# One addition of a weight conversion: VectorE or GpSimd

## The chip, the cores and the metric

The kernel runs on one core of one Trainium2 chip. The metric is the device time of one execution in microseconds, the median of several runs. A core has five engines that run side by side, each through its own list of instructions in order: TensorE (PE, matrix products; PEld is its weight load), VectorE (DVE), ScalarE (ACT), GpSimd (POOL) and SyncE (SP, which here starts the DMA transfers). They meet only through semaphores and memory. SBUF is the on-chip memory that all of them reach, PSUM the memory that TensorE writes its products to.

## What is computed

A gated linear attention and a two-layer network behind it (batch 4, 8 heads, 768 steps, head width 48; network width 384, 2048 inside):

```
for t in range(S):
    state = alpha[:, :, t, :, None] * state + k_t v_t^T
    y[:, :, t] = q_t state
x = y as (3072 tokens, 384)
h = x @ w_in
g = max(0.01 * h, h)
out = g @ w_out
```

The two weights arrive in double precision (64-bit words). The kernel has to turn them into numbers that TensorE can multiply.

## The kernel before, in words

**Products in two halves.** TensorE multiplies in a reduced format, fp32r. Every operand is therefore kept as a high half and a low half: the value rounded to fp32r, and what the rounding left. A product x·w is the sum of three: high·high, low·high and high·low. For the weights the halves of slice f (128 of the 2048 inner columns, 16 slices) lie in one tile `w{f}`, 128 x 768 each: 384 columns of `w_in` and 384 of `w_out`.

**Converting a weight slice.** `converting(f, ordered)` (L240) is a generator. The raw 64-bit words of the slice come by DMA into a tile `raw`. Then, for a slice with `ordered`, each on 128 x 768 elements:

- L259, ScalarE: the top word is scaled as if it were a float.
- L262, ScalarE: a cast of it whose result holds the sign (`signs`).
- L265, VectorE: top word shifted and joined with the sign: `bits`, a float.
- L273, ScalarE: the high half of `w`, rounded from `bits`.
- L277, VectorE: the exponent of `bits` alone, into `pw`.
- L279, VectorE: `bits` minus the high half, in place.
- L281, VectorE: the low word times the exponent, into `rest`, which is `pw` under another name.
- L284, VectorE: `rest` + `val` (which is `bits`) gives the low half of `w`.

Between two of these steps stands a `yield`, so that the caller can put other work between them. `pw` has one buffer (NPW = 1), `bits` two (NBITS = 2), `raw` four.

**Written order.** `put(ordered, eng, op)` (L231) keeps a list for VectorE and one for ScalarE. Each ordered instruction is told to stand behind the last one of its list (`issue_after`), so the order on these two engines is written out by hand. Everything else is put in order by the framework's scheduler, which works from its own estimate of when each instruction could start. The first three slices are converted without that order, in the attention part at the beginning; slices 3 to 15, thirteen, are ordered.

**The items.** The network's work is cut into items (i, f): `ffn_in` takes 384 tokens (block i) through slice f, nine matmuls into a PSUM tile `ph` (two buffers), and makes `gh` and `gl`, the halves of g; `ffn_out`, three items later (LAG = 3), multiplies them with the `w_out` part, nine matmuls. Inside `ffn_in` the steps on the other engines are: L712, ScalarE, t = 0.01 · ph; L715, VectorE, t = max(ph, t); L717, ScalarE, gh; L721, VectorE, gl = t - gh. Blocks 0 and 1 go through the slices together: (0,0), (1,0), (0,1), (1,1) and so on, a pair for each slice. While they do, each pair carries one conversion. The steps are handed out like this (L840 to L845): in an item of block 0, between L717 and L721, L259 of one slice, the last step (L284) of a second and L265 of a third; in an item of block 1, L273 and L277 ahead of L715, then L279 ahead of L721, and L262 and L281 after it. Seen on VectorE, a pair is thus: L281, L715, L284, L265 (next slice), L721, L277, L715, L279, L721, and again L281.

The first matmul of block 0 that uses the low half of slice f comes in the pair after the one in which L284 wrote it.

**Attention between.** The attention of the first nine units (a unit is 128 steps of one batch row) is done at the beginning; the other fifteen are spread between the items by `pace` (L798), which hands out steps by written-down costs. A few of their steps fall among the conversions: transposes (L314), running products (`tensor_tensor_scan`, L339 and L346; through `vector` at L292), and GpSimd's small copies L345 and L351. GpSimd also masks scores (L415) and scales states (L422, a `tensor_tensor` on 192 columns).

Of the kernel before, what the change touches and what calls it, by code (L numbers as in the profile page):

```python
# [17 lines left out]
ALU = mybir.AluOpType  # L18
# [6 lines left out]
def gated_linear_attn_ffn(ctx, tc, q, k, v, alpha, w_in, w_out, out):  # L25
    nc = tc.nc
# [72 lines left out]
    state, vals_sb, rest = rest[:B], rest[B:B + NV], rest[B + NV:]  # L99
# [15 lines left out]
    made = {}  # L115
# [3 lines left out]
    def behind(*key):  # L119

        return tc.issue_after(made[key].ins) if key in made else nullcontext()
# [109 lines left out]
    def put(ordered, eng, op, *args):  # L231

        if not ordered:
            return op(*args)
        line = lines[eng]
        with tc.issue_after(line[-1].ins) if line else nullcontext():
            line.append(op(*args))
        return line[-1]

    def converting(f, ordered=False):  # L240

        if f >= NF:
            return
        raw = jobs.pop(f)
        w_sb[f] = cst.tile([P, 2, 2 * DM], F32R, name=f"w{f}")
        hi, lo = w_sb[f][:, HIGH, :], w_sb[f][:, LOW, :]
        if not f64:
            val = raw[:, :, 0:P].bitcast(F32)
            hi, lo = (t.rearrange("p (g f) -> p g f", f=P) for t in (hi, lo))
            nc.scalar.copy(hi, val)  # L250
            made["w", f] = nc.vector.tensor_tensor(lo, val, hi.bitcast(F32), ALU.subtract)
            return
        words = raw.rearrange("p g (f w) -> p (g f) w", w=2)
        top, low = words[:, :, 1], words[:, :, 0]
        bits = cvp.tile([P, 2 * DM], I32, name="bits", bufs=NBITS)
        val = bits.bitcast(F32)

        with nullcontext() if lines["ACT"] else behind(*AFTER.get(f, ("hi", f - 1))):
            put(ordered, "ACT", lambda: nc.scalar.mul(top.bitcast(F32), top.bitcast(F32), 2.0 ** -112))  # L259
        yield  # L260
        if ordered:
            put(ordered, "ACT", lambda: nc.scalar.copy(  # L262
                signs.bitcast(F16).rearrange("p (n w) -> p n w", w=2)[:, :, 1], top.bitcast(F32)))
            yield
            put(ordered, "DVE", lambda: nc.vector.scalar_tensor_tensor(  # L265
                bits, top, 3, signs, ALU.logical_shift_left, ALU.bitwise_or))
        else:
            with behind("w", f - 1):
                nc.vector.tensor_scalar(bits, top, 3, 0x7FFFFFF8, ALU.logical_shift_left, ALU.bitwise_and)
            yield  # L270
            nc.vector.scalar_tensor_tensor(bits, top, -0x80000000, bits, ALU.bitwise_and, ALU.bitwise_or)
        yield
        made["hi", f] = put(ordered, "ACT", lambda: nc.scalar.copy(hi, val))  # L273
        yield
        pw = cvp.tile([P, 2 * DM], I32, name="pw", bufs=NPW)
        rest = pw.bitcast(F32)
        put(ordered, "DVE", lambda: nc.vector.tensor_scalar(pw, bits, -0x800000, None, ALU.bitwise_and))  # L277
        yield
        put(ordered, "DVE", lambda: nc.vector.tensor_tensor(val, val, hi.bitcast(F32), ALU.subtract))  # L279
        yield  # L280
        put(ordered, "DVE", lambda: nc.vector.scalar_tensor_tensor(  # L281
            rest, low.bitcast(U32), 2.0 ** -52, rest, ALU.mult, ALU.mult))
        yield
        made["w", f] = put(ordered, "DVE", lambda: nc.vector.tensor_tensor(lo, rest, val, ALU.add))  # L284

    def convert(f):
        for _ in converting(f):
            pass
# [485 lines left out]
    for n, _ in enumerate(st):  # L774
        if n == 2:
            load_values(NV - 1)
        while LOADS and LOADS[0][0] in made:
            key, f, part = LOADS.pop(0)
# [8 lines left out]
        if n in STARTS:  # L787
            i, f = items[len(gs)][:2]
# [20 lines left out]
    for n in range(len(items) + LAG):  # L809
        if n < len(items):  # L810
            i, f, _, _ = items[n]
# [21 lines left out]
            if n < len(STARTS):  # L833
                pass
            elif i == 0:
                if coming is None:
                    coming = converting(f + SOON, True)
                    next(coming)
                    next(coming)
                old, new, coming = new or iter(()), coming, converting(f + SOON + 1, True)  # L840
                gs[n] = ffn_in(i, f, (gap1, (coming, old, new) + gap2))
            elif i == 1:
                gs[n] = ffn_in(i, f, ((new, new) + gap1, (new,) + gap2))
                next(coming, None)
                next(new, None)  # L845
            else:
                gs[n] = ffn_in(i, f, (gap1, gap2))
        if n >= LAG:
            i, f, _, tag = items[n - LAG]
# [142 lines left out]
```

## Time and profile before

| what | value |
|---|---|
| median of three runs | 510.71 us (510.24 to 513.04) |
| the profiled execution's own time | 511.59 us |
| its span, first to last instruction | 509.8 us |
| TensorE busy, share of the span | 98% |
| VectorE busy | 73% |
| ScalarE busy | 49% |
| GpSimd busy | 14% |
| L284, one addition on VectorE (mean of 16) | 956 ns |

The profile is of one execution. A line of a view names the line of the program, the engine, the operation, the tile written and the tiles read, and the shapes. In a view by time the first number is the start in us from the span's start and the second the length; "[0.24 <-DVE w L284]" says that the engine was idle for 0.24 us before, until VectorE's instruction of line 284 on tile `w` let it go. VectorE's instructions overlap a little: the next one starts some 0.08 us before the one ahead is noted as ended. In a view by line, "x16 | 15.3, 956 | 0.0" is the count, the total in us, the mean in ns, and the idle time before them. In the waits, "1.0, 1, 1.0" is the total, the number of waits, the longest.

### The profile page before, as it was taken

To read this page: it belongs to the slowest core of one execution; us is meant where nothing else is said; L and a number is where in the kernel's file an instruction comes from. 1 tells how busy PE (TensorE), PEld (TensorE's weight loads), DVE (VectorE), ACT (ScalarE), POOL (GpSimd) and SP (SyncE) were. 2 spreads that over 40 slices of the span, in tenths; PEclk is the share of its full clock that TensorE was granted. 3 is DMA by queue.
4 is the path that set the end of the run, shared out by engine and by line. 5 is a ranking of instruction groups with operands and counts; after the bars stand their busy time and mean duration, and the time that the engine had idled before them with its cause. 6 is when DMAs were issued, how large, how long until landed. Compare 5 with 4: busy or idle time off the path is not lost.

```text
span 509.8 us, 12230 instructions
## 1 busy us (share of the span) xinstructions
PE 497.7 (98%) x4914; PEld 480.5 (94%) x4914; DVE 372.2 (73%) x701; ACT 247.9 (49%) x521; POOL 69.9 (14%) x160
## 2 busy tenths in 40 slices
PE   8998999999999999999999999999999999999996
PEld 7787899999999999999999989999999999999996
DVE  6999999999999768778768578676777674333331
ACT  1765777777655444454343443444444543334331
POOL 5554400000001111111201112102101100000000
PEclk9999999999999999999999999999999999999999
DMA  9999986767204523425225322243421101001001
GB/s 143 167 185 182 211 196 180 213 174 192 31 2 116 148 62 73 111 64 136 52 59 124 91 61 68 64 96 94 101 57 40 42 8 26 1 0 48 1 0 51
DMA packets 92991, 46.77 MB, mean 92 GB/s; under 512 B 57857, under 2 KB 90113, under 8 KB 92929
## 3 DMA queue, kind: packets, MB, share of 16 engines
q1 hardware_dynamic: 92928, 45.93, 41.0%
q8 instruction: 40, 0.66, 0.6%
q14 instruction: 23, 0.18, 0.1%
HBM read 38.83 MB, written 4.72 MB: 85 GB/s over the span
## 4 chain that ended last, share of the span: by engine, by line
PE 84%; DVE 8%; DMA 4%; issue 2%; SPq 1%; ACT 1%; DVEq 0%; POOL 0%; ACTq 0%
PE ph L707 35%; PE b L736 31%; PE a L533 6%; PE a L736 4%; PE b L533 2%; PE a L430 2%; PE ph L533 2%; DMA out_dram<-o 1%; PE b L303 1%; DVE ks L292 1%; DVE qs L292 1%; DMA raw<-in_moe_w_in_dram 1%; DMA large<-large 1%; PE ph L190 1%; DVE rc L292 1%
## 5 line engine op out<-in xcount | busy, mean ns | idle before, releaser
L707 PE MATMUL ph<-large,w 128*128 128x384 f32 x1152 | 225.5, 336 | 1.1 <-DMA large<-large 0.7
L707 PEld LDWEIGHTS ph<-large,w 128*128 128x128 f32 x1152 | 200.4, 188 | 3.2 <-ACT gh L717 1.0
L736 PE MATMUL b<-w,gh 128*128 128x384 f32 x672 | 168.1, 337 | 0.0
L715 DVE TENSOR_TENSOR t<-ph,t 128x384 f32<-128x384 f32 x128 | 70.8, 553 | 71.1 <-ACT t L712 70.9
L736 PEld LDWEIGHTS b<-w,gh 128*128 128x128 f32 x672 | 120.0, 188 | 1.1
L712 ACT ACTIVATE t<-ph 128x384 f32<-128x384 f32 x128 | 62.5, 489 | 113.4 <-PE ph L707 113.2
L717 ACT CAST gh<-t 128x384 fp32r<-128x384 f32 x128 | 65.8, 514 | 99.4 <-DVE t L715 99.3
L736 PE MATMUL b<-w,gl 128*128 128x384 f32 x336 | 108.2, 334 | 0.0
L721 DVE TENSOR_TENSOR gl<-t,gh 128x384 fp32r<-128x384 f32 x128 | 70.9, 554 | 31.2 <-ACT gh L717 31.2
L736 PEld LDWEIGHTS b<-w,gl 128*128 128x128 f32 x336 | 62.7, 188 | 0.0
L415 POOL TENSOR_SCALAR_AFFINE_SELECT sm<-sm 64x256 f32<-64x256 f32 (+1 forms) x48 | 26.1, 552 | 44.9 <-ACT sm L413 39.1
L292 DVE TENSOR_TENSOR_SCAN down<-e,small 128x511 f32<-128x511 f32 x15 | 19.3, 1284 | 7.7 <-DMA out_dram<-o 6.3
L528 POOL MEMSET small<- 128x1 f32 x15 | 1.5, 99 | 152.1 <-PE a L533 149.1
L533 PE MATMUL a<-qs,ks 48*64 48x64 f32 (+1 forms) x552 | 21.2, 228 | 0.8 <-ACT ktok L434 0.5
L292 DVE TENSOR_TENSOR_SCAN up<-e,small 128x128 f32<-128x128 f32 x60 | 20.5, 405 | 0.1
L736 PE MATMUL a<-w,gh 128*128 128x384 f32 x96 | 20.5, 334 | 0.0
L533 PEld LDWEIGHTS a<-qs,ks 48*64 48x64 f32 (+1 forms) x552 | 17.7, 141 | 2.6 <-ACT ktok L434 0.9
L351 POOL COPY small<-up 128x4 f32<-128x4 f32 x15 | 5.9, 392 | 94.1 <-DVE up L292 94.1
L345 POOL COPY down<-small 128x1 f32<-128x1 f32 x15 | 10.8, 723 | 46.7 <-PE b L736 22.2
L736 PEld LDWEIGHTS a<-w,gh 128*128 128x128 f32 x96 | 17.0, 188 | 0.0
L292 DVE STREAM_TRANSPOSE e<-small 128x512 f32<-128x512 f32 x15 | 16.9, 1126 | 0.0
L413 ACT COPY sm<-a 128x256 f32<-128x256 f32 (+1 forms) x24 | 10.8, 449 | 12.5 <-PE b L533 12.5
(110 smaller groups left out, 621.9 us busy)
## 6 DMA issues: line engine op xcount, KB each, us to landing
raw<-in_moe_w_out_dram SPq DMA_DIRECT2D x16, 384.0 KB, 4.1
small<-in_v_dram SPq DMA_DIRECT2D x24, 192.0 KB, 4.1
raw<-in_moe_w_in_dram SPq DMA_DIRECT2D x32, 144.0 KB, 4.2
out_dram<-o SPq DMA_DIRECT2D x24, 192.0 KB, 2.5
small<-in_alpha_dram SPq DMA_DIRECT2D x32, 96.0 KB, 2.4
small<-in_q_dram SPq DMA_DIRECT2D x30, 96.0 KB, 2.2
small<-in_k_dram SPq DMA_DIRECT2D x30, 96.0 KB, 2.2
small<-in_alpha_dram SPq DMA_DIRECT2D x30, 80.0 KB, 2.2
```

Source lines behind the costliest of these rows:

```text
L292: return put(u >= AHEAD, "DVE", lambda: op(*args))
L345: nc.gpsimd.tensor_copy(rc[:, NP - 1, C - 1:C], last)
L413: made["sm", u] = nc.scalar.copy(sm[s], ss[s] if u < AHEAD else within(ss[s]))
L415: made["mask", u] = nc.gpsimd.affine_select(out=sm[s][part], in_=sm[s][part], compare_op=ALU.is_ge, fill=0.0, base=0, pattern=[[0, NP], [1 ...
L430: made["kt", u] = nc.tensor.transpose(kt[:, p * BR:(p + 1) * BR], ks[0:BR, p, :], ident[0:BR, 0:BR])
L533: made["product",] = nc.tensor.matmul(out, weights, moving, start=start, stop=stop, skip_group_check=True)
L707: product = nc.tensor.matmul(ph, w_in_of(f, wn, g), xt[:, g, :], start=n == 0, stop=n == 3 * NG - 1)
L712: put(ordered, "ACT", lambda: nc.scalar.mul(t, ph, 0.01))
L715: put(ordered, "DVE", lambda: nc.vector.tensor_tensor(t, ph, t, ALU.max))
L717: put(ordered, "ACT", lambda: nc.scalar.copy(gh, t))
L721: made["gl", i, f] = put(ordered, "DVE", lambda: nc.vector.tensor_tensor(gl, t, gh.bitcast(F32), ALU.subtract))
L736: product = nc.tensor.matmul(po[j], gt[:, js], w_out_of(f, wn), start=f == 0 and n == 0, stop=f == NF - 1 and n == 2)
```

## The change

For the ordered slices the last addition is issued on GpSimd, outside the written order of VectorE. Both inputs and the output lie in SBUF. The other slices keep VectorE. That the result is noted in `made["w", f]` stays.

```
@@ -281,7 +281,10 @@
         put(ordered, "DVE", lambda: nc.vector.scalar_tensor_tensor(
             rest, low.bitcast(U32), 2.0 ** -52, rest, ALU.mult, ALU.mult))
         yield
-        made["w", f] = put(ordered, "DVE", lambda: nc.vector.tensor_tensor(lo, rest, val, ALU.add))
+        if ordered:
+            made["w", f] = nc.gpsimd.tensor_tensor(lo, rest, val, ALU.add)
+        else:
+            made["w", f] = nc.vector.tensor_tensor(lo, rest, val, ALU.add)
```

## Prediction

> **What bounds the kernel now.** I read the page first (busy time, chain), then the busy time by stage, then the instructions of one conversion in order of time.
>
> ```profile
> span 509.8 us, 12230 instructions
> ```
> ```profile
> PE 497.7 (98%) x4914; PEld 480.5 (94%) x4914; DVE 372.2 (73%) x701; ACT 247.9 (49%) x521; POOL 69.9 (14%) x160
> ```
> ```profile
> PE 84%; DVE 8%; DMA 4%; issue 2%; SPq 1%; ACT 1%; DVEq 0%; POOL 0%; ACTq 0%
> ```
>
> TensorE holds the span and 84% of the chain. VectorE has 8% of the chain, so the question is whether that part lies among the thirteen conversions. The busy time by stage (sum and count in brackets for PE, PEld, DVE, ACT, POOL) says where they are: the ordered additions run from about 75 to 150 us.
>
> ```profile
> 73.00:135.00 62.00, 62.00 (x360) 61.97 (x358) 60.76 (x98) 43.67 (x69) 2.42 (x2) 1.00 0.68 171
> 135.00:152.00 17.00, 16.67 (x93) 15.76 (x92) 16.42 (x27) 10.39 (x18) 0.00 (x0) 1.00 0.01 1
> ```
>
> VectorE is 98% busy there (60.76 of 62.00 us) and TensorE 100%: two engines are full at once. The chain gives TensorE's own pace:
>
> ```profile
> 79.13 1.56 PE ph L707 x9
> ```
> ```profile
> 85.37 1.56 PE ph L707 x9
> ```
>
> Nine matmuls take 1.56 us, 0.173 each, and a pair of items (36 matmuls) comes round every 6.24 us. From 73 to 135 us the 360 matmuls need 62.4 us: nothing is lost. From 135 to 152 us 93 matmuls need 16.1 of 17.0 us: 0.9 us is lost. One loss is the first product of the last converted weight that uses its low half:
>
> ```profile
> 150.54 0.45 PE L707 MATMUL ph<-large,w 128*128 128x384 f32 x1 [0.24 <-DVE w L284]
> ```
>
> So 0.9 us is nearly all that a faster VectorE can give back here, while a slower VectorE has almost no room. Here is one conversion on VectorE, in order of time (start, length):
>
> ```profile
> 85.03 0.95 DVE L281 SCALAR_TENSOR_TENSOR pw<-raw,pw 128x768 f32<-128x768 uint32 x1
> 85.90 0.55 DVE L715 TENSOR_TENSOR t<-ph,t 128x384 f32<-128x384 f32 x1
> 86.37 0.95 DVE L284 TENSOR_TENSOR w<-pw,bits 128x768 fp32r<-128x768 f32 x1
> 87.23 0.95 DVE L265 SCALAR_TENSOR_TENSOR bits<-raw,signs 128x768 int32<-128x768 int32 x1
> 88.10 0.55 DVE L721 TENSOR_TENSOR gl<-t,gh 128x384 fp32r<-128x384 f32 x1
> 88.57 0.55 DVE L277 TENSOR_SCALAR pw<-bits 128x768 int32<-128x768 int32 x1
> ...
> 90.84 0.95 DVE L281 SCALAR_TENSOR_TENSOR pw<-raw,pw 128x768 f32<-128x768 uint32 x1
> 91.71 1.09 DVE L292 STREAM_TRANSPOSE e<-small 128x512 f32<-128x512 f32 x1
> 92.65 0.54 DVE L715 TENSOR_TENSOR t<-ph,t 128x384 f32<-128x384 f32 x1
> ```
>
> Starts follow one another without a gap; a 768-wide instruction takes 0.87 from start to start. One conversion with the work of two items takes 90.84 - 85.03 = 5.81 us against TensorE's 6.24. The difference pays for a few steps of the next attention units (such as the transpose at 91.71).
>
> **What is removed.** Thirteen additions of 0.87 us, 11.3 us of VectorE time, out of a line without gaps.
>
> **What is added: the length of the addition on GpSimd.** The trace has no GpSimd instruction with 768 columns and two inputs. The nearest rows:
>
> ```profile
> L284 DVE TENSOR_TENSOR w<-pw,bits 128x768 fp32r<-128x768 f32 x16 | 15.3, 956 | 0.0
> ```
> ```profile
> L422 POOL TENSOR_TENSOR us<-us,small 112x192 f32<-112x192 f32 x4 | 2.0, 510 | 0.3
> ```
> ```profile
> L528 POOL MEMSET small<- 128x1 f32 x15 | 1.5, 99 | 152.1 <-PE a L533 149.1 <-PE a L865 3.0
> ```
> ```profile
> 30.50 0.19 POOL L351 COPY small<-pc 128x4 f32<-128x4 f32 x1 [0.38 <-DVE pc L292]
> ```
>
> The multiplication of 192 columns takes 0.51. Scaled to 768 with no fixed part: 2.03 us. With the 0.19 of a tiny copy as fixed part: 0.19 + 4 x 0.32 = 1.46. With the 0.10 of a tiny memset: 0.10 + 4 x 0.41 = 1.74, which lies in the middle of the two ends; I take it. Nothing here shows GpSimd writing fp32r, which is a reason to keep the upper end. So the addition goes from 0.95 to about 1.7 us, on an engine that is otherwise nearly idle (2.42 us in the 62).
>
> **What it does to the instructions around it.** The two engines get in each other's way over SBUF. GpSimd and VectorE side by side, before the ordered part:
>
> ```profile
> 44.72 1.57 POOL L415 TENSOR_SCALAR_AFFINE_SELECT sm<-sm 128x512 f32<-128x512 f32 x1 [1.38 <-ACT sm L413]
> ```
> ```profile
> 46.24 0.63 POOL L415 TENSOR_SCALAR_AFFINE_SELECT sm<-sm 128x512 f32<-128x512 f32 x1
> 46.84 1.20 POOL L422 TENSOR_TENSOR small<-small 112x192 f32<-112x192 f32 x1
> ```
> ```profile
> 44.66 0.67 DVE L292 TENSOR_TENSOR large<-b,large 112x512 fp32r<-112x512 f32 x1
> 45.24 0.55 DVE L277 TENSOR_SCALAR pw<-bits 128x768 int32<-128x768 int32 x1
> ...
> 46.30 1.38 DVE L279 TENSOR_TENSOR bits<-bits,w 128x768 f32<-128x768 f32 x1
> 47.60 1.25 DVE L281 SCALAR_TENSOR_TENSOR pw<-raw,pw 128x768 f32<-128x768 uint32 x1
> ```
>
> L279, two SBUF inputs, takes 1.38 instead of 0.95: it ends 0.81 after the select does (46.87 to 47.68). L281 ends 0.81 after the multiplication (48.04 to 48.85). In between the multiplication took 1.20 instead of 0.51: it ended 0.36 after L279, so its wait hid 0.15 of its own length. An instruction that meets the other engine's thus waits for the end of it. L715 and the subtraction at 44.66, with one input in PSUM, are not slowed in these rows. After the change the instructions that can collide with the addition are L265, L721 and L277.
>
> Who goes first? The addition can start about 0.1 after L281 ends (TensorE started 0.06 after L284 ended at 150.48), at 86.08, while L715 runs; without L284 between, L265 would start at 86.37. So GpSimd is 0.3 ahead. But the select at 44.72 was 0.52 ahead of L277, beside an instruction that doesn't collide, and still ended only after L277 (46.29 against 45.79). A second such row:
>
> ```profile
> 59.91 2.24 POOL L415 TENSOR_SCALAR_AFFINE_SELECT sm<-sm 128x512 f32<-128x512 f32 x1
> ```
> ```profile
> 60.25 0.54 DVE L721 TENSOR_TENSOR gl<-t,gh 128x384 fp32r<-128x384 f32 x1
> 60.71 0.95 DVE L284 TENSOR_TENSOR w<-pw,bits 128x768 fp32r<-128x768 f32 x1
> ```
>
> It was 0.34 ahead of L721 and ended 0.49 after L284. VectorE seems to claim its next instruction while the one before still runs. I therefore take it that L265 goes first. Behind L265 the rows are split: at 47.6 GpSimd's multiplication slipped in between two VectorE instructions, at 60.7 its select did not. The multiplication is the nearer row (two inputs, the same conversion's instructions), so I let the addition slip in behind L265.
>
> The Trainium skill (SBUF — State Buffer, "Who interferes with whom") speaks against the change: VectorE with two SBUF inputs and a GpSimd instruction that reads SBUF exclude each other for a whole instruction, and issue order decides who blocks. The trace agrees on the blocking (L279, 1.38 instead of 0.95), less on the order (the select at 44.72). By its order the sum would be 3.8 us instead of 6.2, the second rival below.
>
> One more wait is new: `pw` has a single buffer (NPW = 1), so L277 of the next conversion must wait until GpSimd has read it. Queued behind L277 on VectorE are L715, L279 and L721, and for them wait ScalarE's `gh` and TensorE's next `ph`.
>
> **The sum.** Without the change L277 starts at 88.57. With it: L265 86.37 to 87.32; the addition ends 1.74 - 0.15 = 1.59 later, at 88.91; L721, blocked, ends 0.55 - 0.14 = 0.41 after that, 89.32; L277 starts 0.08 before that end (as 47.60 is before 47.68), 89.24. Each conversion costs VectorE 0.67 us more, not 0.87 less. Eleven conversions have this pattern: 7.4 us. In the one that begins at 90.84 the transpose at 91.71 gives cover: the addition runs 91.89 to 93.63 beside the transpose and L715, L265 ends 0.81 later, so L721 starts at 94.36 where 92.65 + 0.47 + 0.87 + 0.87 = 94.86 was: -0.5. The last of the thirteen:
>
> ```profile
> 148.19 0.95 DVE L281 SCALAR_TENSOR_TENSOR pw<-raw,pw 128x768 f32<-128x768 uint32 x1
> ...
> 149.53 0.95 DVE L284 TENSOR_TENSOR w<-pw,bits 128x768 fp32r<-128x768 f32 x1
> ```
>
> No L265 follows it. The addition would run 149.24 to 150.98 instead of ending at 150.48: +0.5, and TensorE already waits for exactly this. VectorE's idle time in the stretch absorbs something:
>
> ```profile
> DVE down L292 <- PE b L736: 1.0, 1, 1.0
> ```
> ```profile
> DVE t L715 <- ACT t L712: 0.2, 1, 0.2
> ```
>
> That is -1.2. Together 7.4 - 0.5 + 0.5 - 1.2 = 6.2 us. All of it reaches the end: VectorE's cycle becomes 5.81 + 0.67 = 6.48 against TensorE's 6.24; and as TensorE now waits for VectorE's L284 at 150.54, whatever VectorE is late by then TensorE is late too, with nothing but matmul-paced work behind it. GpSimd's own queue adds nothing: the copies L345 and L351 that stand among the additions wait for VectorE instructions that its written order puts ahead. The profiled execution took 511.59 us for its span of 509.8, so it would become 517.8; the median of the three runs is 510.71, and I predict 516.9.
>
> The ends: with 1.46 or 2.03 us for the addition the thirteen change by -0.28 or +0.29 each, -3.6 or +3.8: 2.6 to 10.0 us, 513.3 to 520.7.
>
> **Rivals.**
>
> Addition last: GpSimd loses to L721 too, as the select did at 60.7. Then L721 ends at 87.79, the addition at 89.38, and L277, now waiting for `pw`, starts at 89.44: 0.87 per conversion, 11 x 0.87 - 1.2 = 8.4 us, 519.1; with the long addition 12.2 us, 522.9. For it: two selects out of two lost; against it: the multiplication that won. Chance 0.22.
>
> Addition first: GpSimd holds SBUF from 86.08 to 87.82, L265 ends 0.81 later, L721 starts at 88.55 instead of 88.10: 0.45 each, 11 x 0.45 - 1.2 = 3.8 us, 514.5; with the short addition 0.1 us, 510.8. This is the order that the Trainium skill's page SBUF — State Buffer gives. For it: a lead of 0.3 us; against it: the select at 44.72. Chance 0.20.
>
> No harm, and a gain: the blocking doesn't touch these instructions. VectorE saves 0.87 and loses 0.2 waiting for `pw` (addition ends 87.82, L277 wants 87.70 and starts near 87.9), some 8 us in all; TensorE, the bound again, gets back at most its 0.9: 509.8. It turns on whether L265 runs at 0.95 beside the addition. L279 at 46.30 speaks against it. Chance 0.15, almost all of it within 0.5%.
>
> My forecast: chance 0.33. What is left, 0.10, goes to a longer addition (fp32r rounding) and to another order of the instructions that are not written out.
>
> **How the numbers follow.** 0.5% is 2.55 us, about what a measurement of this kernel can tell from no change; slower means above 513.3. My forecast (nearly all of it), the addition last, three quarters of the addition first and most of the rest: 0.77. Within 0.5%: no harm, the rest of the addition first: 0.19. Faster: 0.04, by a luckier order alone. The range runs from the addition first at its short end, 510.8, to the addition last at its long end, 523.0; it leaves out no harm (0.15) and about half of the rest.
>
> **What would show it.** In the changed profile: the addition on GpSimd of 1.5 to 2.0 us when alone and over 2.5 from start to end where it waits for L265; L721 or L265 far longer than 0.55 or 0.95 (above 1.5); VectorE's cycle near 6.5 us; TensorE idle by 0.2 to 0.3 us in every pair, put down to the addition's `w` or to `t`, from about 85 us on. I am wrong if L265, L721 and L277 keep their lengths and the cycle falls to 5.2, or if the addition takes under 1.2 us.

## The result, and the profile after

| kernel | median of 7 runs | range |
|---|---|---|
| before | 512.27 us | 510.24 to 513.25 |
| changed | 516.96 us | 514.76 to 520.51 |

The ratio is 1.0087, with a 95% interval of 1.0058 to 1.0115: the changed kernel is slower, by 3.0 to 5.9 us. More runs of the kernel before moved its median from 510.71 to 512.27, so the rise is 4.7 us where 6.2 was forecast; that the forecast time of 516.9 looks exact is luck, as worked out further down.

The profiled execution of the changed kernel took 520.51 us, the slowest of its seven, for a span of 518.8. Part of that has nothing to do with the change: its granted clock was 0.83 from 40 to 60 us, ahead of the ordered conversions. I therefore compare the stretch of the conversions, from the first ordered L281 to the last, and not the spans. In the changed file all lines behind the edit are three further on: L715 is L718, L721 is L724, and the addition is L285.

First the busy time by stage. Columns as before: PE, PEld, DVE, ACT, POOL, each with its count.

```profile
75.86:138.00 62.14, 61.03 (x346) 59.24 (x345) 62.11 (x81) 41.55 (x68) 19.72 (x11) 1.00 0.66 165
138.00:158.50 20.50, 18.03 (x99) 16.75 (x98) 19.76 (x28) 10.70 (x18) 6.72 (x4) 1.00 0.00 0
```

VectorE has 17 instructions fewer than before in the same time (81 instead of 98 in some 62 us) and is noted as busy for all of it: 62.11 of 62.14. TensorE has gaps now. The view by time shows what VectorE is busy with, one conversion:

```profile
82.21 0.94 DVE L281 SCALAR_TENSOR_TENSOR pw<-raw,pw 128x768 f32<-128x768 uint32 x1
83.08 0.55 DVE L718 TENSOR_TENSOR t<-ph,t 128x384 f32<-128x384 f32 x1
83.55 2.35 DVE L265 SCALAR_TENSOR_TENSOR bits<-raw,signs 128x768 int32<-128x768 int32 x1
85.82 0.55 DVE L724 TENSOR_TENSOR gl<-t,gh 128x384 fp32r<-128x384 f32 x1
86.29 0.55 DVE L277 TENSOR_SCALAR pw<-bits 128x768 int32<-128x768 int32 x1
86.76 0.54 DVE L718 TENSOR_TENSOR t<-ph,t 128x384 f32<-128x384 f32 x1
87.23 0.94 DVE L279 TENSOR_TENSOR bits<-bits,w 128x768 f32<-128x768 f32 x1
88.09 0.54 DVE L724 TENSOR_TENSOR gl<-t,gh 128x384 fp32r<-128x384 f32 x1
88.57 0.94 DVE L281 SCALAR_TENSOR_TENSOR pw<-raw,pw 128x768 f32<-128x768 uint32 x1
```

and GpSimd in the same stretch:

```profile
83.24 1.84 POOL L285 TENSOR_TENSOR w<-pw,bits 128x768 fp32r<-128x768 f32 x1 [4.50 <-DVE pw L281]
```

The addition starts 0.09 us after L281's end at 83.15, beside L718, and runs undisturbed for 1.84 us to 85.08. L265 is noted from 83.55, but it ends 0.82 us after the addition, at 85.90: it stood blocked for 1.4 us. "Busy" here is mostly waiting. The cycle from L281 to L281 is 88.57 - 82.21 = 6.36 us instead of 5.81. By line, the exchange is plain: thirteen additions of 0.95 us left VectorE, and the thirteen L265 grew by 1.23 us on average, from 962 to 2191 ns. (The first L265 stands ahead of the first addition and is not blocked; the last addition blocks L724 instead.) L265 before, then L265 and the addition after:

```profile
L265 DVE SCALAR_TENSOR_TENSOR bits<-raw,signs 128x768 int32<-128x768 int32 x13 | 12.5, 962 | 0.0
```
```profile
L265 DVE SCALAR_TENSOR_TENSOR bits<-raw,signs 128x768 int32<-128x768 int32 x13 | 28.5, 2191 | 0.0
```
```profile
L285 POOL TENSOR_TENSOR w<-pw,bits 128x768 fp32r<-128x768 f32 x13 | 24.0, 1846 | 60.0 <-DVE pw L281 60.0
```

The exception is the pair with a transpose ahead of L718, which gives cover:

```profile
94.92 0.95 DVE L281 SCALAR_TENSOR_TENSOR pw<-raw,pw 128x768 f32<-128x768 uint32 x1
95.79 1.09 DVE L295 STREAM_TRANSPOSE e<-small 128x512 f32<-128x512 f32 x1
96.72 0.54 DVE L718 TENSOR_TENSOR t<-ph,t 128x384 f32<-128x384 f32 x1
97.19 1.42 DVE L265 SCALAR_TENSOR_TENSOR bits<-raw,signs 128x768 int32<-128x768 int32 x1
```

L265 waits 0.5 us only. That cycle took 6.71 us before and takes 6.36 now.

TensorE's waits between 70 and 165 us say where the loss lands:

```profile
PE b L739 <- DVE gl L724: 1.5, 2, 0.9
PE ph L710 <- DVE t L718: 1.2, 3, 0.8
PE ph L710 <- POOL w L285: 0.9, 1, 0.9
```

Before, the whole list was one wait:

```profile
PE ph L707 <- DVE w L284: 0.2, 1, 0.2
```

These waits are not the whole loss. Between the first ordered L281 and the last, TensorE is noted as busy for 76.96 us with 434 matmuls, where it was 74.70 us with 432 before; two matmuls are worth 0.35 us, so some 1.9 us more stand inside its busy time. The last of the waits is the product that waits for the last slice's low half:

```profile
158.29 1.49 PE L710 MATMUL ph<-large,w 128*128 128x384 f32 x7 [0.85 <-POOL w L285]
```

### The profile page after: what moved, and what is told of

Same layout as the page of the kernel before. It is cut to its first block, busy times and chain, and to the rows that moved or that the text cites. A ratio compares the mean times of both kernels' runs of the same rounds, so it can differ in the third digit from the quotient of the medians.

```text
span 518.8 us, 12265 instructions
## 1 busy us (share of the span) xinstructions
PE 501.5 (97%) x4914; PEld 482.7 (93%) x4914; DVE 378.1 (73%) x688; ACT 247.2 (48%) x521; POOL 90.9 (18%) x173
## 4 chain that ended last, share of the span: by engine, by line
PE 54%; DVE 3%; DMA 2%; issue 1%; ACT 1%; SPq 1%; DVEq 0%; POOL 0%; ACTq 0%
PE b L739 24%; PE ph L710 24%; PE a L536 4%; DMA out_dram<-o 1%; DVE qs L295 1%; PE ph L536 1%; DVE ks L295 1%; PE a L433 1%; DMA large<-large 1%; DVE gl L724 0%; SPq L157 0%; DVE t L718 0%; DVE e L295 0%; ACT ktok L437 0%; ACT gh L720 0%
## 5 line engine op out<-in xcount | busy, mean ns | idle before, releaser
L718 DVE TENSOR_TENSOR t<-ph,t 128x384 f32<-128x384 f32 x128 | 70.2, 549 | 69.2 <-ACT t L715 69.1
L715 ACT ACTIVATE t<-ph 128x384 f32<-128x384 f32 x128 | 62.6, 489 | 112.6 <-PE ph L710 109.9
L724 DVE TENSOR_TENSOR gl<-t,gh 128x384 fp32r<-128x384 f32 x128 | 71.1, 555 | 31.9 <-ACT gh L720 31.8
L285 POOL TENSOR_TENSOR w<-pw,bits 128x768 fp32r<-128x768 f32 x13 | 24.0, 1846 | 60.0 <-DVE pw L281 60.0
L265 DVE SCALAR_TENSOR_TENSOR bits<-raw,signs 128x768 int32<-128x768 int32 x13 | 28.5, 2191 | 0.0
L273 ACT CAST w<-bits 128x768 fp32r<-128x768 f32 x16 | 13.4, 836 | 8.8 <-DVE bits L265 7.4
```

The lines of the kernel that those rows point to most:

```text
L265: put(ordered, "DVE", lambda: nc.vector.scalar_tensor_tensor(bits, top, 3, signs, ALU.logical_shift_left, ALU.bitwise_or))
L285: made["w", f] = nc.gpsimd.tensor_tensor(lo, rest, val, ALU.add)
L715: put(ordered, "ACT", lambda: nc.scalar.mul(t, ph, 0.01))
L718: put(ordered, "DVE", lambda: nc.vector.tensor_tensor(t, ph, t, ALU.max))
L724: made["gl", i, f] = put(ordered, "DVE", lambda: nc.vector.tensor_tensor(gl, t, gh.bitcast(F32), ALU.subtract))
```

## The experiments

Theory A, formed from this profile: GpSimd, first by 0.3 us, holds SBUF for the whole of its addition, and L265, which reads two SBUF inputs, is blocked until the end. The rivals are B, the new wait for `pw`; C, a low half that reaches TensorE later because GpSimd is slower; D, merely another order of the instructions that are not written out. Times are medians, beside runs of the kernel before on the same chip. "Stretch" is the time from the first ordered L281 to the last in the profile: 74.79 us before, 79.50 in the changed kernel.

**The changed kernel again.**

> The changed kernel once more, on one chip with the other runs. Theory A (GpSimd takes SBUF first and holds it for its 1.85 us, L265 waits 1.4 of it): 0.54 us more on VectorE per conversion, VectorE's cycle 6.35 us, the time 3.5 to 6 us over the kernel before. The rivals (B: the new wait for pw; C: the low half reaches TensorE later; D: only another order of the instructions) say the same here.

517.48 us against 512.56, ratio 1.0078 (1.0055 to 1.0101), stretch 79.53, at a granted clock of 0.999. The stretch agrees with the first profile to 0.03 us, so the 0.83 of clock ahead of it did not touch it.

**Two buffers for `pw`.**

```
-    NBITS, NPW, NRAW = 2, 1, 4
+    NBITS, NPW, NRAW = 2, 2, 4
```

> The changed kernel with two buffers for pw (NPW = 2), so that L277 no longer waits for GpSimd. Theory A: L277 never waited, as L265 is held until the addition is done; time as the changed kernel, 3.5 to 6 us over before, L265 still near 2.35 us. Theory B: the loss goes away, within 1 us of before.

516.92 us, 1.0082 (1.0053 to 1.0110). L265 is as long as in the changed kernel:

```profile
L265 DVE SCALAR_TENSOR_TENSOR bits<-raw,signs 128x768 int32<-128x768 int32 x13 | 28.5, 2196 | 0.0
```

The edit tests less than it seems to. In the built programs the framework lays `pw` of successive slices at two alternating places in SBUF although NPW is 1; only two pairs of successive ordered slices share a place in the changed kernel, and with NPW = 2 there are again two. What puts rival B out is the trace of the changed kernel: no L277 waited for GpSimd there, since the addition, which went first, was over by then.

**No addition at all.** L281 writes the low half of `w` itself, so one term of it is left out in thirteen slices.

```
-            rest, low.bitcast(U32), 2.0 ** -52, rest, ALU.mult, ALU.mult))
+            lo, low.bitcast(U32), 2.0 ** -52, rest, ALU.mult, ALU.mult))
+        yield
+        return
```

> The thirteen ordered additions are left out on both engines (L281 writes the low half itself, so the low half lacks one term): the most that taking them from VectorE could ever give. VectorE's cycle 5.81 - 0.87 = 4.94 us, less than TensorE's 6.24, so TensorE is the bound. Theory A, by the window from 135 to 152 us: 0.5 to 1.2 us under before. If VectorE held more than that window showed, 3 us or more under before.

511.77 us, 0.9980 (0.9965 to 0.9995): 0.3 to 1.8 us under before. So leaving the additions out altogether wins about a microsecond, as TensorE's 0.9 us of loss said. Hardly any of the 11.3 us of VectorE time was on the path. VectorE's cycle fell to 5.26 us at the least, not to 4.94: between 70 and 160 us it now waits 6.0 us for ScalarE's `t`.

**VectorE first.** The addition is given a wait for the next slice's L265.

```
+            for g, add in late:
+                made["w", g] = add()
+                waits_for(made["w", g], ahead)   # ahead: the next slice's L265
```

> The addition waits until the next slice's L265 has ended (except for the last slice), so VectorE goes first, as the prediction had it. L721 then runs ahead of it, L277 waits for pw: about 1.05 us per conversion more than before, 11 to 13 us over before, L265 back at 0.95 us. If only the latency to TensorE mattered (C), about 1 us later in each pair but no more than the 6 to 8 us that this adds up to after the free time of a pair.

520.35 us, 1.0143 (1.0115 to 1.0171): 7.8 us over before, less than the 11 to 13 expected. VectorE, then GpSimd (in this file L265 is L267, L721 is L734, L277 is L283):

```profile
87.18 0.94 DVE L267 SCALAR_TENSOR_TENSOR bits<-raw,signs 128x768 int32<-128x768 int32 x1
88.05 0.55 DVE L734 TENSOR_TENSOR gl<-t,gh 128x384 fp32r<-128x384 f32 x1
88.51 2.21 DVE L283 TENSOR_SCALAR pw<-bits 128x768 int32<-128x768 int32 x1
```
```profile
88.20 2.10 POOL L291 TENSOR_TENSOR w<-pw,bits 128x768 fp32r<-128x768 f32 x1 [4.50 <-DVE bits L267]
```

L265 is back at 0.94. GpSimd arrives while the subtraction L734 runs, waits about 0.25 us for its end, and then L283 is the one that is blocked, 1.7 us long. It has a single SBUF input; it also passes its 768 columns in 0.55 us where those with two inputs take 0.95, and whether the two are connected was not tried. L283 is noted as started at 88.51, before the addition's end at 90.30: it was held in SBUF, not at a semaphore for `pw`, and it ends 0.42 us after the addition. Ten of the L283 are like this one. Only one, in the single pair of ordered slices whose `pw` share a place in this kernel, stood at the semaphore; it ends 0.60 after the addition's end at 138.64:

```profile
138.68 0.56 DVE L283 TENSOR_SCALAR pw<-bits 128x768 int32<-128x768 int32 x1 [1.74 <-POOL w L291]
```

The missing wait is thus worth 0.18 us per conversion, some 2 of the 3 to 5 us by which my expectation was too high; the rest was not traced. The cycle is 6.6 us, 0.8 over before. Going second is dearer than going first (0.55), so the order matters. In these conversions the addition, which starts 0.3 us ahead of L283, goes ahead of it. In the first conversion it starts just as far ahead and goes behind:

```profile
75.41 2.57 POOL L291 TENSOR_TENSOR w<-pw,bits 128x768 fp32r<-128x768 f32 x1 [13.14 <-DVE bits L267]
```
```profile
75.71 0.56 DVE L283 TENSOR_SCALAR pw<-bits 128x768 int32<-128x768 int32 x1
```

There a later VectorE instruction, L285 (L279 in the kernel before), is the one that is blocked, 1.83 us long. Why this one addition lost is open.

**Busy, but reading nothing.** GpSimd writes zeros over the low half two and a half times; thirteen low halves are left out of the products.

```
+            for n, part in enumerate((lo, lo, lo[:, 0:DM])):
+                made["w", f] = nc.gpsimd.memset(part.bitcast(F32), 0.0)   # the first waits for L281
```

> In place of the addition GpSimd fills the low half with zeros, two and a half times, so that it is busy about 1.85 us after L281 but reads nothing from SBUF (the low halves of thirteen slices are left out of the products). Theory A, the collision is one of reads: L265 back near 0.95 us, VectorE's cycle under 5.1 us, time 0 to 1.5 us under before. If GpSimd's being busy or the later low half (C) is what costs: as the changed kernel, 3.5 to 6 us over before.

510.46 us against 513.03, 0.9950 (0.9928 to 0.9972), 1.4 to 3.7 us under before. The cycle falls to 5.27 us at the least, not under 5.1. GpSimd is busy for 2.0 us and L265 runs beside it at its own length:

```profile
85.27 2.02 POOL L286 MEMSET w<- 128x768 f32 x3 [3.31 <-DVE pw L281]
```
```profile
86.57 0.95 DVE L265 SCALAR_TENSOR_TENSOR bits<-raw,signs 128x768 int32<-128x768 int32 x1
```

Rival C is out: a low half that comes from GpSimd just as late costs nothing. The collision is one of reads. The Trainium skill (SBUF — State Buffer, "Who interferes with whom") says so: VectorE with two SBUF inputs contends with a GpSimd instruction that reads SBUF, not with one that only writes it. The 0.95 here against the 2.35 in the changed kernel agrees. This kernel wins 2.6 us where the one without any addition won 0.8, which was not expected; the two intervals overlap only from 1.4 to 1.8 us. So what freeing VectorE returns is known to a microsecond or two, not better.

**Twice the cost.** The addition is issued twice.

> The addition is done twice on GpSimd, same inputs and output. Theory A: it holds SBUF 1.8 us longer, L265 about 4.1 us, cycle 8.1 us, 13 x 1.8 = 23 us over the changed kernel, 26 to 30 us over before. If VectorE gets in between the two (L265 between them), L265 2.35 and L721 or L277 wait: about the same total. Theory D (order only): as the changed kernel.

542.27 us, 1.0566 (1.0537 to 1.0595): 29 us over before, in the range of A. D is out: one GpSimd instruction more per conversion moves the time by 25 us over the changed kernel. The changed kernel's own trace says the same: TensorE's order differs from before in places, but VectorE has the same instructions in the same order, less the thirteen additions, and is idle for 0.14 of the 79.50 us of the stretch, so the stretch is as long as VectorE makes it. The blocking goes in turns:

```profile
91.16 1.85 POOL L285 TENSOR_TENSOR w<-pw,bits 128x768 fp32r<-128x768 f32 x1 [3.64 <-DVE pw L281]
93.08 2.42 POOL L286 TENSOR_TENSOR w<-pw,bits 128x768 fp32r<-128x768 f32 x1
```
```profile
91.47 2.35 DVE L265 SCALAR_TENSOR_TENSOR bits<-raw,signs 128x768 int32<-128x768 int32 x1
93.74 2.17 DVE L725 TENSOR_TENSOR gl<-t,gh 128x384 fp32r<-128x384 f32 x1
```

The first addition blocks L265; L265, already waiting, goes ahead of the second addition; that in turn goes ahead of L725 and blocks it.

**Half on each engine.** Columns 0 to 383 on GpSimd, the rest on VectorE ahead of L265.

```
+            put(ordered, "DVE", lambda: nc.vector.tensor_tensor(lo[:, DM:], rest[:, DM:], val[:, DM:], ALU.add))
+            made["w", f] = nc.gpsimd.tensor_tensor(lo[:, 0:DM], rest[:, 0:DM], val[:, 0:DM], ALU.add)
```

> Columns 0 to 383 of the low half on GpSimd, 384 to 767 on VectorE ahead of L265. GpSimd's half, by 0.51 us for 192 columns and 1.85 for 768, takes 0.96. Theory A: it ends about 2.0 us after L281's start, VectorE's half, due at 1.34, ends near 2.4: 0.1 us more per conversion than before, the time within 1.5 us of before. If holding SBUF weren't the cause, VectorE would save 0.4 us per conversion: 0.5 to 1 us under before.

512.43 us, 0.9983 (0.9965 to 1.0001), within the 1.5 us that A gave; at 0.6 us under before it also lies in the rival's 0.5 to 1, so the time doesn't tell them apart. The rows do. VectorE's half, alone some 0.55 us, takes 1.12, as it starts while GpSimd's half runs:

```profile
88.97 1.02 POOL L286 TENSOR_TENSOR w<-pw,bits 128x384 fp32r<-128x384 f32 x1 [4.97 <-DVE pw L281]
```
```profile
89.28 1.12 DVE L285 TENSOR_TENSOR w<-pw,bits 128x384 fp32r<-128x384 f32 x1
```

The cycle is 5.99 us from L281 to L281, 0.18 over before where 0.1 was expected. Moving half the addition wins nothing either.

**Who goes first.** My prediction held that VectorE claims its next instruction while the one before still runs. To ask this directly, an extra VectorE sum of a constant tile with itself stands between L715 and L265, with no wait for another engine.

```
             made["w", f] = nc.gpsimd.tensor_tensor(lo, rest, val, ALU.add)
+            put(ordered, "DVE", lambda: nc.vector.tensor_tensor(blank, plain, plain, ALU.add))
```

> Asks who goes first. The changed kernel with one more VectorE instruction of 0.95 us between L715 and L265, where L284 stood: the sum of a constant tile with itself, with no wait for a semaphore of another engine. If an instruction without such waits is claimed for VectorE while L715 runs, as the prediction had it, it takes 0.95 us, the addition goes behind it, and L265 is the long one or not. If the first to start wins, as in the changed kernel, it takes about 2.35 us and L265 0.95. Either way the cycle is about 0.87 us longer than 6.35, some 10 us over the changed kernel.

```profile
89.51 0.54 DVE L722 TENSOR_TENSOR t<-ph,t 128x384 f32<-128x384 f32 x1
89.98 2.36 DVE L289 TENSOR_TENSOR blank<-plain 128x768 f32<-128x768 f32 x1
92.26 0.95 DVE L268 SCALAR_TENSOR_TENSOR bits<-raw,signs 128x768 int32<-128x768 int32 x1
```
```profile
89.67 1.85 POOL L288 TENSOR_TENSOR w<-pw,bits 128x768 fp32r<-128x768 f32 x1 [5.37 <-DVE pw L284]
```

The extra sum takes 2.36 us, the addition 1.85: the first to start wins, 0.31 us ahead, even against an instruction that has nothing to wait for. VectorE has no claim at this place. One execution took 530.57 us. The cycle is 7.22 us, the changed kernel's 6.36 and 0.87 for the extra sum, and the stretch is 89.67, 10.2 more than the changed kernel's.

**Is it the kind of GpSimd instruction?** The rows that misled me were affine selects. Two kernels put a select of 768 columns in the addition's place (the addition is left out), one of them with the extra sum.

```
+            made["w", f] = nc.gpsimd.affine_select(
+                out=lo, in_=val, compare_op=ALU.is_ge, fill=0.0, base=0, pattern=[[1, 2 * DM]], channel_multiplier=0)
```

> Why the selects before the ordered part lost to VectorE though they started first, while the addition wins. In place of the addition GpSimd copies val to the low half by an affine select of 768 columns with one input (the addition is left out), behind L281 as the addition is. If it is the kind of GpSimd instruction, the select loses here too: L265 0.95 us, the select near 2 us or more (alone about 0.9 to 1.2 us, by 0.63 for 512 columns). If it is something at that earlier place, the select wins: L265 about 1.6 us, the select 0.9 to 1.2.

> The select in place of the addition (which is left out), and the extra VectorE sum of a constant tile ahead of L265, which waits for no other engine. If VectorE's claim on its next instruction needs one without waits and a select on the other side: the extra sum takes 0.95 us and the select waits for it. If neither matters: the extra sum takes about 1.6 us, the select 0.9 to 1.2.

```profile
86.39 0.83 POOL L285 TENSOR_SCALAR_AFFINE_SELECT w<-bits 128x768 fp32r<-128x768 f32 x1 [4.49 <-DVE pw L281]
```
```profile
86.72 1.32 DVE L265 SCALAR_TENSOR_TENSOR bits<-raw,signs 128x768 int32<-128x768 int32 x1
```

The select wins as the addition does, with 0.83 us in every conversion, under the 0.9 to 1.2 estimated, and L265 is 0.37 longer where it starts this close behind the select. With the extra sum, this sum takes 1.30 us on average and the select again 0.83. One execution each took 514.39 and 515.06 us. So a select as such does not lose; it was something else at that earlier place.

## Why the prediction was right and wrong

**Right: the bound.** TensorE's 0.9 us of loss in the stretch was given as the most that VectorE could return. Without the addition on either engine 0.8 us is returned (0.3 to 1.8). The kernel that fills with zeros returned 2.6 (1.4 to 3.7), so the bound holds in its size and not to the tenth.

**Right: that the two engines block each other, and its cost.** L279's 1.38 us, read from before, gave the rule that a blocked 768-wide instruction ends 0.81 us after the other engine. L265 ends 0.82 after the addition.

**Nearly right: the length of the addition.** 1.74 us was taken, between 1.46 and 2.03; it is 1.85.

**Wrong: "I therefore take it that L265 goes first".** The addition goes first, in all thirteen conversions. The case that came is the rival "addition first", which had a chance of 0.20 and 514.5 us. This is also the order of the Trainium skill (SBUF — State Buffer, "Who interferes with whom"), by which issue order decides; I had weighed that rule against the select at 44.72 and let the select win. The additional sum with no wait, 2.36 us long, settles for the rule at this place. It is not the whole rule: one addition of the kernel with VectorE first lost though it started ahead, and what the selects met stays open. In the changed kernel, too, one loses that started 0.2 us ahead.

```profile
61.90 2.12 POOL L418 TENSOR_SCALAR_AFFINE_SELECT sm<-sm 128x512 f32<-128x512 f32 x1 [5.54 <-ACT sm L416]
```
```profile
61.51 0.68 DVE L295 TENSOR_TENSOR large<-b,large 112x512 fp32r<-112x512 f32 x1
62.11 0.55 DVE L724 TENSOR_TENSOR gl<-t,gh 128x384 fp32r<-128x384 f32 x1
62.58 0.95 DVE L287 TENSOR_TENSOR w<-pw,bits 128x768 fp32r<-128x768 f32 x1
```

It ended 0.5 us after L287. In all three places (44.72 and 59.91 before, 61.90 here) VectorE's instruction on `large` was already running when the select started, at 59.91 this one:

```profile
59.65 0.68 DVE L292 TENSOR_TENSOR large<-b,large 112x512 fp32r<-112x512 f32 x1
```

The prediction took it for one that doesn't collide because it was not slowed; that doesn't show that it leaves GpSimd alone. Whether it matters was not tried.

**Wrong: the wait for `pw`.** The prediction, and the description of the kernel before, took NPW = 1 for one buffer. The built programs have two alternating places for `pw`, but for one or two pairs of slices. In the changed kernel L277 never stood at a semaphore for it, as the addition, going first, is over before L277 comes. Where the addition goes second, L277 is held in SBUF ten times (2.2 us) and stands at the semaphore once (1.74 us).

**The sum, term by term.** With the addition first I gave 0.45 us per conversion, 11 of them, -0.5 for the one with the transpose, +0.5 for the last and -1.2 of idle time absorbed: 3.8. The 0.11 us by which the addition is longer adds 1.4 over thirteen: 5.2. The profiles show: 0.55 in most conversions (6.36 - 5.81), the one with the transpose 6.36 instead of 6.71 (-0.35), the one with the long scan and VectorE's idle time 8.10 instead of 8.71, which is +0.55 less 1.2 absorbed; the stretch 79.50 instead of 74.79, +4.7. The last addition ends 2.88 us after its L281 started (155.36 to 158.24) where L284 ended 2.29 after (148.19 to 150.48), +0.6. That is 5.3 us by the profiles, against 4.7 (3.0 to 5.9) in time. My forecast's 0.67 per conversion was the price of the wrong case. That it gave 516.9 is luck: a rise 1.5 us too large was added to a median of before that was, with three runs, 1.6 us lower than with seven.

**Partly right: the signs.** L265 beyond 1.5 us and a long cycle were there; the cycle was 6.36, not 6.5. TensorE's idle time is not spread at 0.2 to 0.3 us over the pairs but falls in six waits, 3.6 us together, the last for `w`; what is lost besides is noted as busy.

## What to carry to other kernels

Moving an elementwise instruction that reads SBUF from VectorE to GpSimd frees no time on VectorE, as far as these runs show, when its neighbours there read two SBUF tensors, or are like L277, which was blocked with one: the neighbour waits for the whole of the slower instruction. Before moving, list what VectorE does in the next two microseconds behind the moved instruction's input, and count as cover only what did not lengthen beside GpSimd, here the instruction with one input in PSUM (0.47 us) and the transpose (0.93). And ask first what the freed time is worth: VectorE was busy for 98% of a stage here, and taking 11.3 us from it returned 0.8 in one kernel and 2.6 in another. And look where the tiles lie before counting on a wait for a buffer: the count in the program was 1, and the framework used two places.

## What the runs showed of the hardware that was not expected

- When GpSimd has two instructions ready, the engines take turns: in the kernel with two additions a VectorE instruction that was already blocked went in between, and the second addition took 2.42 us instead of 1.85.
- Who goes first is not settled by the start alone: by its 0.3 us of lead the addition goes ahead in the changed kernel and with the extra sum, but with as much lead one addition (75.41) and two selects of before (0.34 and 0.52) went behind.
- A blocked instruction is noted as busy. VectorE's 62.11 of 62.14 us hold some 1.4 us of waiting in most of the conversions; only the length by line gives it away (2.19 us on average instead of 0.96).
- A `tensor_tensor` of 768 columns with an fp32r result takes 1.85 us on GpSimd, of 384 columns 1.02: 2.16 ns a column and 0.19 us besides. A select of 768 columns takes 0.83.
